# Four experts' results turned into rows by VectorE and transfers instead of TensorE, and the surplus plan moved into the last expert's phase

## The chip, the cores and the metric

The kernel runs on one core of a Trainium2 chip. The metric is device time in microseconds (us) of one execution; lower is better. The core's engines are TensorE (matrix products; its weight loads are listed apart as PEld), VectorE (DVE), ScalarE (ACT), GpSimd (POOL) and SyncE (SP), which here only issues transfers. Each engine works through its own instructions in order and waits for the others by semaphores.

## The reference, cut to what matters

Attention comes first, with a mask by hash buckets; it is untouched here. Its output, 3072 tokens of 512 numbers, goes through a mixture of eight experts. Each token is sent to the one expert with the largest logit:

```python
logits = x @ w_gate                      # x: 3072 x 512, 8 experts
expert_idx = np.argmax(logits, axis=1)
perm = np.argsort(expert_idx, kind='stable')
x_sorted = x[perm]
for e in range(8):
    lo, hi = boundaries[e], boundaries[e + 1]
    h = np.maximum(x_sorted[lo:hi] @ w1[e], 0.0)     # 512 -> 1024
    y_sorted[lo:hi] = h @ w2[e]                      # 1024 -> 512
y = y_sorted[inv_perm]
return gate_w[:, None] * y
```

## The kernel before

The first 400 us are attention and routing. They leave the tokens sorted by expert in a DRAM tensor (`sorted_rows`). What follows is a loop over phases `n` = 1 to 8 (phase 0 overlaps the end of attention). The experts are ranked by their number of tokens. Phases 0 and 1 are two halves, of 256 tokens, of the largest; phases 2 to 8 are the other seven, with room for 456, 432, 408, 396, 384, 372 and 354 tokens (`CAPS`). Tokens beyond that room are the surplus. A plan (`spill_plan`: some 46 small VectorE instructions, written as a generator that is advanced step by step) lists them in a small DRAM table, and a loop at the very end, run as many times as the plan says, works them off.

A phase has two parts. In the first, `mm1(n, f)` for f = 0 to 7 makes 128 hidden features of all the tokens: 12 products, since numbers are split into a high and a low part and three of the four combinations are summed. ScalarE writes the relu's high part (`relu("u")`), VectorE its low part (`relu("d")`), both out of one of three PSUM buffers (`s`). In the second part, `mm2(n, m)` for m = 0 to 3 multiplies by the second weights. Phases with at most 384 tokens are `by_token`: there a product's result has tokens in its rows and can be multiplied by the gate and scattered to the output (`yout`). In phases 2 to 5 the result comes out turned, with 128 output features in the rows and tokens in the columns. ScalarE copies it to the tile `yt`, and in the next phase's first part, after every second `mm1`, TensorE turns 128 tokens of it by four transposes (line 889), VectorE multiplies by the gate (line 894) and GpSimd scatters the rows by an indirect transfer (line 896).

Beside this the next expert is prepared. `halves` calls `chunk_part` once for each `mm1` and twice for each `mm2`: ScalarE rounds 512 columns of raw weights to their high part (line 718), GpSimd subtracts for the low part (line 719), and after each second part SyncE issues the load of another half chunk of raw weights (line 705), three halves ahead of its use. `rows` loads the next expert's tokens (line 735), 32 rows at a time, and `xt_blocks` turns them by VectorE's transposes of 32 x 32 blocks (line 773). The order on each engine is the order in which the program is written.

Of the kernel before, what the change touches and what calls it, by code (L numbers as in the profile page):

```python
# [7 lines left out]
F32 = mybir.dt.float32  # L8
# [15 lines left out]
E = 8  # L24
# [29 lines left out]
@with_exitstack  # L54
def lsh_attention_moe(ctx, tc, qk, qk2, v, proj, wg, w1, w1p, w2, out):
    nc = tc.nc
# [543 lines left out]
    def spill_plan():  # L600
# [18 lines left out]
        nc.vector.tensor_tensor(over, C["cnt"], cap, op=OP.subtract)  # L619
        gt = m2.tile([128, E, 21], F32, name="gt")  # L620
        yield
# [54 lines left out]
        nc.vector.tensor_scalar(tab[:, :, 1], et, float(E - 1), None, op0=OP.min)  # L676
        nc.sync.dma_start(tabd.rearrange("t p c -> p t c"), tab)
        cnt = const.tile([1, 1], I32, name="spn")
# [8 lines left out]
    def raw_load(c, a):  # L687

        r, k = divmod(c, 4)
        if k < 2:  # L690
            src = (w1p if r else w1)[bass.ds(EV[r], 1)].rearrange("o (a p) f -> p (o a) f", p=128)[:, 2 * a:2 * a + 2,
                                                                                k * 512:(k + 1) * 512]
        else:
            o = (k - 2) * 4 + 2 * a
            src = w2[bass.ds(EV[r], 1)].rearrange("o (a p) d -> p (o a) d", p=128)[:, o:o + 2, :]
        n = 2 * c + a
        if n in (2, 3):
            if n == 2:
                RAW["x"] = moe.tile([128, 2, 2, 512], F32, name="xhe")
            t = RAW["x"][:, a]  # L700
        elif n < 10 or n % 2:
            t = moe.tile([128, 2, 512], F32, name="raw", bufs=2)
        else:
            t = P2["p"].tile([128, 2, 512], F32, name="raw2", bufs=2)
        nc.sync.dma_start(t, src)
        RAW[c, a] = t
# [137 lines left out]
    def mm2(n, m, mid=None):  # L844

        r, o, c = PH[n]
        if by_token(n):
            yout(n, m, mid)
            return
        if m == 0:  # L850
            YT[n] = (wk.tile([128, 4, EARLY], F32, name="qk") if n == 0 else
                     P2["p"].tile([128, 4, CAPS[1]], F32, name="yt"))
        h = HH[n]
        ms = slice(m * 128, (m + 1) * 128)
        p = ps.tile([128, 512], F32, name="s", bufs=3)
        k = 0
        for f in range(8):
            w = CH[4 * r + 2 + f // 4]
            for a, b in ((0, 0), (0, 1), (1, 0)):
                nc.tensor.matmul(p[:, :c], w[:, a, f % 4, ms], h[b][:, f, :c], start=(k == 0), stop=(k == 23))  # L860
                k += 1
                if k == 12 and mid:
                    mid()
        nc.scalar.activation(YT[n][:, m, :c], p[:, :c], AF.Copy)

    def yout(n, j, mid=None):
# [4 lines left out]
        if n + 1 == len(PH) and j + 1 == len(tiles_of(c)):  # L871
            youts(n, j, i, pw)
            return
        p = ps.tile([128, 512], F32, name="s", bufs=3)
        if by_token(n):
            k = 0
            for f in range(8):
                w = CH[4 * r + 2 + f // 4]
                for a, b in ((0, 0), (1, 0), (0, 1)):
                    nc.tensor.matmul(p[:pw], HH[n][b][:, f, i:i + pw], w[:, a, f % 4],  # L880
                                     start=(k == 0), stop=(k == 23))
                    k += 1
                    if k == (12 if n else 20) and mid:
                        mid()
        else:

            yw = max(pw, min(128, CAPS[1] - i))
            for m in range(4):
                nc.tensor.transpose(p[:yw, m * 128:(m + 1) * 128], YT[n][:, m, i:i + yw], ident)  # L889
        if n:  # L890
            y = P2["p"].tile([128, DM], F32, name="y", bufs=3)
        else:
            y = moe.tile([128, DM], F32, name="y0")
# [8 lines left out]
    def youts(n, j, i, pw):  # L902

        r = PH[n][0]
        y = P2["p"].tile([128, DM], F32, name="y", bufs=3)
        ix = P2["p"].tile([128, 2], I32, name="ix2")
# [274 lines left out]
    for n in range(1, len(PH)):  # L1181
        c0 = 4 * (PH[n][0] + 1)
        last = n + 1 == len(PH)
        if not last:
            rows(n + 1)
        for f in range(8):
            mm1(n, f)
            if f % 2 and not by_token(n - 1):
                yout(n - 1, f // 2)
            halves(c0, f)  # L1190
            if 3 <= n < 6:
                for _ in range(2):
                    next(plan, None)
        for m in range(4):
            if not last:
                xt_blocks(n + 1, ((0, 1), (2,), (3,), ())[m] if not by_token(n) else ((0, 1), (2, 3), (), ())[m])
            if not (last and m == 3):
                mm2(n, m)
            halves(c0 + 2, 2 * m)
            halves(c0 + 2, 2 * m + 1)  # L1200
        if n == 6:
            for _ in plan:
                pass
        if n == 7:
            C["n"] = nc.values_load(C["cntn"][0:1, 0:1], min_val=0, max_val=TMAX)
    p2.close()
# [67 lines left out]
```

## Time and profile before

| | |
|---|---|
| median of three runs | 699.95 us (699.9 to 700.3) |
| the profiled execution | 699.71 us |
| its span, first to last instruction | 697.8 us |
| granted TensorE clock | 0.999 of full speed |
| TensorE busy | 688.8 us, 99% of the span |
| VectorE, ScalarE, GpSimd busy | 64%, 62%, 67% |

A share of busy time is an average over the whole span; what a change is worth is read from the stretch in which it is made, here from about 440 us to the end.

### The profile page before, as it was taken

The page shows a single profiled execution, that of the slowest core. Times are in us where ns is not written, and L with a number is a line of the kernel's source. Part 1 is how long each engine was busy: PE and PEld are TensorE (multiplying, and loading weights), DVE is VectorE, ACT ScalarE, POOL GpSimd, SP SyncE. Part 2 cuts the span into 40 slices and gives each one's busy share as a digit, 9 for nine tenths or more (in the row PEclk, how much of TensorE's full clock was granted, in tenths as well). Part 3 has the DMA queues.
Part 4 walks back from the last instruction along what each step waited for, and adds up shares of the span by engine and source line. Part 5 has one row for each costly group of instructions (what it writes and reads, how often), then busy time and mean ns, then how long its engine had stood idle before and what let it go on. Part 6 is the DMA issues. An engine that isn't in the chain of part 4 may idle for free.

```text
span 697.8 us, 12285 instructions
## 1 busy us (share of the span) xinstructions
PE 688.8 (99%) x4219; PEld 564.7 (81%) x4219; DVE 444.6 (64%) x916; ACT 434.3 (62%) x866; POOL 466.8 (67%) x517
## 2 busy tenths in 40 slices
PE   8999999999999999999999999999999999999997
PEld 4778677867786778677876789899999999989896
DVE  8878787878787878788875645342939333363421
ACT  7988888878888888887876315443443444444310
POOL 7967755595796768876866436856666676758522
PEclk9999999999999999999999999999999999999999
DMA  7609777976778558764983158656355493738101
GB/s 285 160 19 261 208 219 210 269 187 219 254 230 222 154 132 224 223 202 143 257 274 129 65 184 248 170 177 155 127 163 170 131 181 123 210 124 234 61 10 42
DMA packets 64528, 123.09 MB, mean 176 GB/s; under 512 B 15329, under 2 KB 29025, under 8 KB 64400
## 3 DMA queue, kind: packets, MB, share of 16 engines
q1 hardware_dynamic: 56736, 103.17, 52.2%
q0 software_dynamic: 7584, 19.10, 8.6%
q8 instruction: 34, 0.56, 0.3%
q14 instruction: 30, 0.25, 0.1%
q10 hardware_dynamic: 144, 0.02, 0.0%
HBM read 65.75 MB, written 26.33 MB: 132 GB/s over the span
## 4 chain that ended last, share of the span: by engine, by line
PE 92%; issue 4%; POOL 1%; ACT 1%; DVE 1%; POOLq 0%
PE s L823 19%; PE t L389 18%; PE s L860 11%; PE s L297 10%; PE t L327 10%; PE s L299 9%; PE s L880 8%; PE t L409 3%; PE t L254 2%; PE s L889 1%; POOL w L719 1%; PE t L103 1%; ACT e L313 0%; POOL out_dram L896 0%; ACT pt L379 0%
## 5 line engine op out<-in xcount | busy, mean ns | idle before, releaser
L307 DVE TENSOR_SCALAR_CACHE_REDUCE e<-s 128x768 f32<-128x768 f32 x192 | 178.9, 953 | 61.3 <-PE s L299 56.5
L313 ACT ACTIVATE e<-e,m 128x768 f32<-128x768 f32 x192 | 177.9, 929 | 16.3 <-DVE e L307 12.4
L719 POOL TENSOR_TENSOR w<-raw,w 128x512 fp32r<-128x512 f32 x112 | 144.6, 1314 | 36.7 <-ACT w L718 35.5
L389 PE MATMUL t<-pt,vt 128*64 128x384 f32 x768 | 130.9, 490 | 0.0
L823 PE MATMUL s<-xh,w 128*128 128x456 f32 (+6 forms) x672 | 126.8, 346 | 0.0
L823 PEld LDWEIGHTS s<-xh,w 128*128 128x128 f32 x672 | 119.2, 188 | 3.0
L839 DVE SCALAR_TENSOR_TENSOR hh<-s,hh 128x256 fp32r<-128x256 f32 (+7 forms) x64 | 35.5, 555 | 107.5 <-ACT hh L837 107.5
L389 PEld LDWEIGHTS t<-pt,vt 128*64 128x64 f32 x768 | 52.3, 137 | 63.7 <-issue 63.2
L327 PE MATMUL t<-ident,e 128*128 128x128 f32 x648 | 92.1, 274 | 1.4 <-DVE pt L377 0.5
L379 ACT ACTIVATE pt<-t 128x512 f32<-128x512 f32 (+1 forms) x147 | 82.1, 581 | 16.4 <-PE t L327 15.3
L837 ACT ACTIVATE hh<-s 128x256 fp32r<-128x256 f32 (+7 forms) x64 | 31.3, 490 | 90.7 <-PE s L823 90.7
L327 PEld LDWEIGHTS t<-ident,e 128*128 128x128 f32 x648 | 76.6, 140 | 8.7 <-ACT e L313 1.8
L349 DVE STREAM_TRANSPOSE w<-e 128x768 f32<-128x768 f32 x84 | 79.0, 964 | 0.8 <-DMA pt<-w 0.6
L896 POOL DMA_INDIRECT out_dram<-y,ix x28 | 27.9, 996 | 73.1 <-DVE y L894 43.9
L860 PE MATMUL s<-hh,w 128*128 128x456 f32 (+3 forms) x384 | 74.9, 355 | 0.0
L860 PEld LDWEIGHTS s<-hh,w 128*128 128x128 f32 x384 | 71.1, 188 | 2.6
L718 ACT ACTIVATE w<-raw 128x512 fp32r<-128x512 f32 x112 | 66.3, 622 | 1.0 <-DMA raw<-in_w1p_dram 1.0
L880 PE MATMUL s<-w,hh 128*128 128x512 f32 (+1 forms) x240 | 56.4, 394 | 0.0
L297 PE MATMUL s<-w 80*128 80x384 f32 x192 | 55.1, 368 | 0.0
L297 PE MATMUL s<-qk 80*128 80x384 f32 x192 | 54.8, 367 | 0.0
L880 PEld LDWEIGHTS s<-w,hh 128*128 128x128 f32 (+1 forms) x240 | 44.6, 187 | 10.5
L299 PE MATMUL s<-qk 128*128 128x384 f32 x192 | 49.8, 340 | 0.0
(220 smaller groups left out, 979.9 us busy)
## 6 DMA issues: line engine op xcount, KB each, us to landing
pt<-w SPq DMA_DIRECT2D x224, 144.0 KB, 3.8
raw<-in_w_dram SPq DMA_DIRECT2D x34, 512.0 KB, 3.4
raw<-in_w1p_dram SPq DMA_DIRECT2D x28, 512.0 KB, 3.4
xd<-in_qk_dram SPq DMA_DIRECT2D x14, 768.0 KB, 7.1
sorted_rows<-xr SPq DMA_DIRECT2D x6, 1156.0 KB, 8.1
vt<-in_v_dram SPq DMA_DIRECT2D x16, 384.0 KB, 3.8
masks<-bits POOLq DMA_DIRECT2D x14, 192.0 KB, 3.8
sorted_rows<-sorted_rows SPq DMA_DIRECT2D x2, 1156.0 KB, 7.1
```

The costliest lines, as they stand in the source:

```text
L297: nc.tensor.matmul(p[:, a, :HALF], k[0:80, 2, c], k[0:80, 3, n], start=i >= 4, stop=i < 4)
L299: nc.tensor.matmul(p[:, a, :HALF], k[:, 0, c], k[:, 1, n], start=i < 4, stop=i >= 4)
L307: nc.vector.tensor_scalar(e, SC.pop(i)[:, :, :HALF], CEIL, None, op0=OP.min, op1=OP.min, accum_out=m)
L313: nc.scalar.activation(e, e, AF.Exp, bias=m, scale=-1.0, accum_out=SM[g, hf][:, t, s:s + 1])
L327: nc.tensor.transpose(o[:, j, w], e[w][:, kt // 3, (kt % 3) * 128:(kt % 3) * 128 + 128], ident)
L349: nc.vector.transpose(z[:, :, c, w].rearrange("p g (k i) -> p g k i", i=32), e)
L379: nc.scalar.activation(o, x, AF.Copy)
L389: nc.tensor.matmul(p[s * 64:(s + 1) * 64, :HALF], VT[g][:, kt, s, :], PT[u][:, :, :, s, kt].rearrange("p a t i -> p t a i"), start=(kt == ...
L719: nc.gpsimd.tensor_tensor(w[:, 1, a], r, w[:, 0, a], op=OP.subtract)
L823: nc.tensor.matmul(p[:, :c], w[:, a, d, fs], x[:, b, d, :c], start=(k == 0), stop=(k == 11))
L860: nc.tensor.matmul(p[:, :c], w[:, a, f % 4, ms], h[b][:, f, :c], start=(k == 0), stop=(k == 23))
L880: nc.tensor.matmul(p[:pw], HH[n][b][:, f, i:i + pw], w[:, a, f % 4], start=(k == 0), stop=(k == 23))
```

## The change

In phases 2 to 5 the turning of the results leaves TensorE. After each `mm2` VectorE turns the copy `yt` by 32 x 32 blocks into a new tile `yb`. Such a transpose moves nothing between groups of 32 partitions; that is left to 16 transfers (`y_rows`), each from 32 partitions of `yb` to 32 of a new tile `yr`, in pieces of 512 bytes. SyncE issues two of them after each of the next phase's eight `mm1`. For the pieces to be whole, these four experts' second weights are read from a new input `w2p` with permuted columns. The multiplication by the gate now reads and writes `yr` in place, and it and the scatter stand in the next phase's second part, one behind each `mm2`. GpSimd clears the last columns of `yt` once a phase. The fourth block of the next expert's tokens is turned one `mm2` earlier.

The surplus plan was advanced by two steps behind each `mm1` of phases 3 to 5 and finished after phase 6. It is now advanced by six steps behind each of the last six `mm1` of phase 8; its table is stored after that phase's first `mm2`, and the number of turns is read by all the engines after its second.

```diff
@@ spill_plan
-        gt = m2.tile([128, E, 21], F32, name="gt")
+        gt = m2.tile([128, E, 24], F32, name="le2")[:, :, :21]
...
-        nc.sync.dma_start(tabd.rearrange("t p c -> p t c"), tab)
+        C["tab"] = tab
@@ raw_load
-            src = w2[bass.ds(EV[r], 1)].rearrange("o (a p) d -> p (o a) d", p=128)[:, o:o + 2, :]
+            src = (w2 if r == 0 or by_token(r + 1) else w2p)[bass.ds(EV[r], 1)].rearrange("o (a p) d -> p (o a) d", p=128)[:, o:o + 2, :]
@@ mm2
+        nb = -(-c // 32)
         if m == 0:
-            YT[n] = (wk.tile([128, 4, EARLY], F32, name="qk") if n == 0 else
-                     P2["p"].tile([128, 4, CAPS[1]], F32, name="yt"))
+            YT[n] = P2["p"].tile([128, 4, CB * 32], F32, name="yt")
+            YB[n] = P2["p"].tile([128, CB, 128], F32, name="yb")
+            nc.gpsimd.memset(YT[n][:, :, c:nb * 32], 0.0)
...
         nc.scalar.activation(YT[n][:, m, :c], p[:, :c], AF.Copy)
+        nc.vector.transpose(YB[n][:, :nb, 32 * m:32 * m + 32], YT[n][:, m, :nb * 32].rearrange("p (b j) -> p b j", j=32))
+
+    YB, YR = {}, {}
+
+    def y_rows(n, k):
+
+        nb = -(-PH[n][2] // 32)
+        if k == 0:
+            YR[n] = P2["p"].tile([128, 4, DM], F32, name="yr")
+        for i in (2 * k, 2 * k + 1):
+            r, a = divmod(i, 4)
+            q = (a + r) % 4
+            t = len(range(q, nb, 4))
+            nc.sync.dma_start(YR[n][32 * q:32 * q + 32, :t, 128 * a:128 * a + 128], YB[n][32 * a:32 * a + 32, q::4][:, :t])
@@ yout
-        p = ps.tile([128, 512], F32, name="s", bufs=3)
         if by_token(n):
+            p = ps.tile([128, 512], F32, name="s", bufs=3)
...
         else:
-
-            yw = max(pw, min(128, CAPS[1] - i))
-            for m in range(4):
-                nc.tensor.transpose(p[:yw, m * 128:(m + 1) * 128], YT[n][:, m, i:i + yw], ident)
-        if n:
-            y = P2["p"].tile([128, DM], F32, name="y", bufs=3)
+            p = YR[n][:, j]
+        if not by_token(n):
+            y = p
+        elif n:
+            y = P2["p"].tile([128, DM], F32, name="y", bufs=2)
@@ the loop over phases
         for f in range(8):
             mm1(n, f)
-            if f % 2 and not by_token(n - 1):
-                yout(n - 1, f // 2)
             halves(c0, f)
-            if 3 <= n < 6:
-                for _ in range(2):
-                    next(plan, None)
+            if not by_token(n - 1):
+                y_rows(n - 1, f)
+            if last and f > 1:
+                go(plan, 6)
         for m in range(4):
             if not last:
-                xt_blocks(n + 1, ((0, 1), (2,), (3,), ())[m] if not by_token(n) else ((0, 1), (2, 3), (), ())[m])
+                xt_blocks(n + 1, ((0, 1), (2, 3), (), ())[m])
             if not (last and m == 3):
                 mm2(n, m)
+            if not by_token(n - 1):
+                yout(n - 1, m)
             halves(c0 + 2, 2 * m)
             halves(c0 + 2, 2 * m + 1)
-        if n == 6:
-            for _ in plan:
-                pass
-        if n == 7:
-            C["n"] = nc.values_load(C["cntn"][0:1, 0:1], min_val=0, max_val=TMAX)
+            if last and m == 0:
+                go(plan, 99)
+                nc.sync.dma_start(tabd.rearrange("t p c -> p t c"), C["tab"])
+            if last and m == 1:
+                C["n"] = nc.values_load(C["cntn"][0:1, 0:1], min_val=0, max_val=TMAX)
```

TensorE's order in the first products of phase 3, before (`xh` holds that expert's tokens, `w` its first weights, `yt` the turned result of phase 2; line 860 is the second products):

```order
L823 MATMUL s<-xh,w_5362 128x432 x24
L889 MATMUL s<-ident,yt 128x128 x4
L823 MATMUL s<-xh,w_5362 128x432 x24
L889 MATMUL s<-ident,yt 128x128 x4
L823 MATMUL s<-xh,w_5435 128x432 x24
L889 MATMUL s<-ident,yt 128x128 x4
L823 MATMUL s<-xh,w_5435 128x432 x24
L889 MATMUL s<-ident,yt 72x128 x4
```

In the changed program the four groups of transposes are gone there, and the same 96 products follow each other without a break.

SyncE's queue in phase 3 after the change, behind the load of the next tokens (`xg` is its last piece, `raw` the raw weights; line 880 is `y_rows`):

```order
L740 DMA xg<-sorted_rows 128x4x2
L880 DMA yr<-yb 32x4x128 x2
L705 ISA
L705 DMA raw<-in_w1p_dram 128x2x512
L880 DMA yr<-yb 32x4x128
L880 DMA yr<-yb 32x3x128
L880 DMA yr<-yb 32x4x128 x2
L705 ISA
L705 DMA raw_5735<-in_w2p_dram 128x2x512
```

Before, the loads of raw weights followed the line of `xg` directly; now the first of them stands behind two transfers of rows and each later one behind four.

VectorE's order in the first products of phase 8 after the change (line 839 is `relu("d")`, lines 625 to 644 are the plan):

```order
L839 SCALAR_TENSOR_TENSOR hh_7305<-s,hh_7304 128x354
L625 TENSOR_REDUCE spl<-le_7377 128x8
L627 COPY spl<-spl 128x8
L630 TENSOR_TENSOR spl<-spl 128x1 x4
L839 SCALAR_TENSOR_TENSOR hh_7305<-s,hh_7304 128x354
L630 TENSOR_TENSOR spl<-spl 128x1 x3
L640 TENSOR_TENSOR le<-spl,tf 128x192
L642 TENSOR_REDUCE ttt<-le 128x24
L644 TENSOR_TENSOR le<-le,spl 128x192
L839 SCALAR_TENSOR_TENSOR hh_7305<-s,hh_7304 128x354
```

Before, the eight relus of this phase stood there one after the other, and these plan rows stood in phases 3 to 5 (the storing of the table in phase 6).

## Rows read from the trace of the kernel before

**Rows 1.** The page: its engines, and the chain that ended last.

```profile
PE 688.8 (99%) x4219; PEld 564.7 (81%) x4219; DVE 444.6 (64%) x916; ACT 434.3 (62%) x866; POOL 466.8 (67%) x517
...
PE s L823 19%; PE t L389 18%; PE s L860 11%; PE s L297 10%; PE t L327 10%; PE s L299 9%; PE s L880 8%; PE t L409 3%; PE t L254 2%; PE s L889 1%; POOL w L719 1%; PE t L103 1%; ACT e L313 0%; POOL out_dram L896 0%; ACT pt L379 0%
```

**Rows 2.** Stretches: phase 3's first products, its second, phase 8's first.

```profile
core 0: us, PE busy (x) PEld busy (x) DVE busy (x) ACT busy (x) POOL busy (x), PEclk, DMA share, GB/s
478.79:499.29 20.50, 20.50 (x113) 19.47 (x112) 14.05 (x33) 9.10 (x18) 13.63 (x18) 1.00 0.67 183
499.29:518.27 18.98, 18.98 (x100) 18.15 (x97) 9.74 (x16) 7.57 (x15) 11.51 (x10) 1.00 0.36 117
660.45:676.03 15.58, 15.58 (x98) 15.58 (x96) 4.44 (x8) 3.27 (x7) 6.36 (x6) 1.00 0.05 11
```

**Rows 3.** The chain in order of time: start us, us, what.

```profile
478.95 4.71 PE s L823 x24
483.66 0.44 PE s L889 x4
...
499.54 18.89 PE s L860 x96
...
643.88 16.73 PE s L880 x72
```

**Rows 4.** Line 889's instructions: min/median/max ns, first and last start us.

```profile
L889 PE MATMUL s<-ident,yt x64: 270/272/275, 483.5 to 610.7; 128*128 128x128 f32 x48, 128*72 128x128 f32 x16
```

**Rows 5.** VectorE from 418 us, by line and shape: busy us, mean ns.

```profile
L894 DVE TENSOR_SCALAR y<-s,gate 128x512 f32<-128x512 f32 x21 | 15.6, 744 | 18.5 <-PE s L880 18.5
...
L773 DVE STREAM_TRANSPOSE xt<-xb 128x480 f32<-128x480 f32 x4 | 2.5, 650 | 0.0
```

**Rows 6.** VectorE in order of time: start us, us, instruction.

```profile
501.75 0.15 DVE L630 TENSOR_TENSOR spl<-spl 128x1 f32<-128x1 f32 x1
501.93 0.36 DVE L640 TENSOR_TENSOR le<-spl,tf 128x192 f32<-128x192 f32 x1
...
536.52 2.88 DVE L667 TENSOR_SCALAR ttt<-ttt,rof 128x24 f32<-128x24 f32 x1
...
666.99 0.53 DVE L839 SCALAR_TENSOR_TENSOR hh<-s,hh 128x354 fp32r<-128x354 f32 x1 [1.42 <-ACT hh L837]
```

**Rows 7.** GpSimd in order of time; in brackets idle time before.

```profile
483.88 0.16 POOL L110 IOTA kf_i<- 128x21 int32 x1
...
536.80 2.55 POOL L719 TENSOR_TENSOR w<-raw,w 128x512 fp32r<-128x512 f32 x2
...
663.04 5.03 POOL L719 TENSOR_TENSOR w<-raw,w 128x512 fp32r<-128x512 f32 x4
...
682.86 1.00 POOL L896 DMA_INDIRECT out_dram<-y,ix  x1 [14.75 <-DVE y L894]
...
691.29 0.98 POOL L923 DMA_INDIRECT out_dram<-y,ix  x1 [1.90 <-DVEq L1210]
```

**Rows 8.** SyncE's queue in order of time, start of phase 4.

```profile
522.16 0.39 SPq L705 DMA_DIRECT2D raw<-in_w1p_dram  x1
```

**Rows 9.** ScalarE in order of time, phase 4.

```profile
518.47 0.53 ACT L864 ACTIVATE yt<-s 128x432 f32<-128x432 f32 x1 [3.15 <-PE s L860]
...
535.89 0.62 ACT L718 ACTIVATE w<-raw 128x512 fp32r<-128x512 f32 x1
```

**Rows 10.** Transfers by tile: KB each, median us from issue to landing.

```profile
raw<-in_w1p_dram SPq DMA_DIRECT2D x28, 512.0 KB, 3.4
...
xb<-sorted_rows SPq DMA_DIRECT2D x8, 208.0 KB, 5.0
...
spill_rows<-tab SPq DMA_DIRECT2D x1, 24.0 KB, 9.1
```

**Rows 11.** The scatters of tile y, issue to landing.

```profile
DMA to landing us min/median/max: 1.9/2.8/8.8
```

**Rows 12.** The read of the number of turns: ns, start us.

```profile
L1205 PEldq TENSOR_LOAD <-spn x1: 484/484/484, 656.3 to 656.3; - x1
...
L1205 POOLq TENSOR_LOAD <-spn x1: 502/502/502, 661.7 to 661.7; - x1
```

More of the change, by code (lines that the diff above doesn't have):

```diff
@@ L54, in lsh_attention_moe @@
 @with_exitstack
-def lsh_attention_moe(ctx, tc, qk, qk2, v, proj, wg, w1, w1p, w2, out):
+def lsh_attention_moe(ctx, tc, qk, qk2, v, proj, wg, w1, w1p, w2, w2p, out):
     nc = tc.nc
@@ L904, in youts @@
         r = PH[n][0]
-        y = P2["p"].tile([128, DM], F32, name="y", bufs=3)
+        y = P2["p"].tile([128, DM], F32, name="y", bufs=2)
         ix = P2["p"].tile([128, 2], I32, name="ix2")
@@ L1262 @@
     w1 = np.ascontiguousarray(w1).reshape(E, DM, F)
+    w2p = np.ascontiguousarray(np.asarray(inputs["moe_w2"]).reshape(E, F, 4, 4, 32).transpose(0, 1, 3, 2, 4)).reshape(E, F, DM)
     pj, wg = pj.reshape(2 * D, 32), wg.reshape(2 * D, NP, 2 * E)
@@ L1265 @@
               "in_w1_dram": np.ascontiguousarray(inputs["moe_w1"]), "in_w1p_dram": w1,
-              "in_w2_dram": np.ascontiguousarray(inputs["moe_w2"])}
+              "in_w2_dram": np.ascontiguousarray(inputs["moe_w2"]), "in_w2p_dram": w2p}
     nc = bacc.Bacc("TRN2", target_bir_lowering=False, num_devices=1, dynamic_dma_scratch_size=2048)
```

## Prediction

> **What bounds the kernel now.** I read the page first. TensorE is busy for 99% of the span and holds 92% of the chain that ended last [rows 1], so the end moves with TensorE's own work, unless the change makes TensorE wait. The chain's lines then say where in the span to look: line 889, the transposes that the change takes out, stands among TensorE's lines with 1% [rows 1]. The view by stretches comes next. I cut it at the starts of the first products (line 823) and second products (line 860) of each phase. In every stretch the granted clock is 1.00 of 2.4 GHz and TensorE is busy for the whole stretch, while VectorE, ScalarE and GpSimd are each busy for well under it [rows 2]. A list of TensorE's waits from 418 us on is empty. So in this stretch of the program one microsecond less of TensorE work is one microsecond less of span, as long as the other engines stay ahead.
>
> **What is removed.** 64 transposes: four phases (3 to 6, each turning the result of the one before), four tiles of tokens each, four transposes a tile. Their price depends on the view. The list of instructions gives each 272 ns [rows 4], but matmuls overlap in the array, so durations can't be added. The chain counts each instruction by what it adds to the end: a group of four takes 0.44 us between two runs of 24 products that take 4.71 us [rows 3]. 16 such groups are 7.0 us. The stretches give a second reading. The first products of phase 3 (96 of 432 columns, with four groups) take 20.50 us and its second products (96 of 432 columns, without) 18.98 [rows 2]: 1.52 us a phase, 6.1 us for four. This reading is low, since it is cut at starts: the products behind the last group begin while it still drains. In the chain, which counts ends, the same two stretches are 499.54 - 478.95 = 20.59 us and 18.89 us [rows 3], 1.70 apart, or 6.8 us for four. I take 7.0 and keep 6.1 as the low bound.
> The Trainium skill (TensorE: Matmul & The Clock Gate, Part 4: PE-mode transpose) gives about 275 ns for a transpose in a kernel's context. The trace agrees on the duration (272 ns), but by that price the sum would be 64 x 0.272 = 17.4 us, and by the chain it is 7.0; the two stretches above, 1.5 us apart and not 16 x 0.272 = 4.4, decide for the chain.
>
> **What is added on VectorE.** 16 transposes of blocks of up to 480 columns in the second products. The like of them, on 128x480, takes 650 ns [rows 5]. Each waits for ScalarE's copy of the result (0.53 us [rows 9]). Behind the one after the last second product stand one multiplication by the gate and the next expert's first relu. The multiplication (744 ns out of PSUM [rows 5]) now reads and writes SBUF. Its price there isn't in the trace; I bound it from 0.2 us to 2.9 us. The upper end is a small instruction within SBUF that took 2.88 us [rows 6], while GpSimd ran two subtractions of weights from 536.80 for 2.55 us and both ended at 539.4 [rows 7]. At worst VectorE is free 0.53 + 0.65 + 2.9 = 4.1 us into the next phase and ends its first relu 0.6 us later, at 4.7. A group of 12 first products takes 4.71 / 2 = 2.35 us in phase 3 [rows 3] and 384/432 of that, 2.1, in phase 6; with three PSUM buffers the fourth group is the first to want that buffer, 3 x 2.1 = 6.3 us in. So it costs nothing, and 1.6 us of delay are left before it does.
> The Trainium skill (SBUF — State Buffer, Who interferes with whom) has VectorE and GpSimd lock one pair of ports, the second blocked until the first is done. The trace agrees at the pair of rows that end at 539.4. By that rule the 16 multiplications would lose up to 16 x 2.2 = 35 us of VectorE's time, and TensorE none of it as long as each loss ends within those 1.6 us.
>
> **What is added on SyncE.** 16 transfers in each of phases 3 to 6, 64 KB at most each, on the queue that also loads raw weights. The nearest transfers take 5.0 us to land (208 KB, pieces of 512 bytes), raw weights 3.4 [rows 10]. Together they are 4 MB more, in stretches where the DMA engines are busy for 0.67 and 0.36 of the time [rows 2]. The first two of a phase write the tile of rows that the phase before still scatters. In phases 4 to 6 this makes the queue wait until that last scatter has landed: 0.53 + 0.65 + 0.2 to 2.9 on VectorE, 1.0 for the scatter's issue [rows 7], 2.8 for its landing (8.8 at most [rows 11]), 5.2 to 13.9 us after the phase began. Behind stands a load of raw weights that is issued today 3.9 us after the start of phase 4 (522.16 - 518.27 [rows 2, 8]). ScalarE needs it for its copy at 535.89 [rows 9], 17.6 us in. With 3.4 us of landing it may be issued as late as 14.2. So the wait is hidden, by nearly all of its bound.
> The scatters move from the first products to the second, four a phase. GpSimd's work, 16 subtractions of 5.03 / 4 = 1.26 us [rows 7] and four scatters of 1.0, is 24 us of 39.5 in phase 3 (20.50 + 18.98 [rows 2]), as before. Some subtractions slip by a few microseconds, and their weights are wanted half a phase later. Price: nothing.
>
> **What is moved.** The surplus plan goes from phases 3 to 5 into the last one, phase 8, six steps behind each of its last six first relus, where it is about 46 small VectorE instructions. Undisturbed ones take 0.15 to 0.36 us [rows 6]; some 12 are of the dear kind, 8 are memsets, the rest cheap: about 9 us by this estimate. The plan starts once GpSimd has ended the last subtractions at 663.04 + 5.03 = 668.07 and three index rows of 0.16 [rows 7], 8 us after phase 8 began (660.45). A group of first products takes 15.58 / 8 = 1.95 us [rows 2], and today the third relu runs at 666.99 [rows 6], before that point. With 1 to 2 us of plan between two relus of 0.53 us, the fourth relu ends near 10.3 us, when its buffer is wanted at 11.7; the sixth near 14.0, wanted at 15.6; the eighth near 18.4. That one is wanted by the 23rd or 24th of the second products, and 72 of those take 16.73 us [rows 3]: 15.58 + 23 x 0.232 = 20.9. TensorE waits for none, with 1.4 us to spare at the tightest. The spill count is ready at 19.3. TensorE's queue reads it ahead of the last half tile's products, which start at 15.58 + 48 x 0.232 = 26.7; today it reads it (0.48 us) at 656.3, 4.1 us before the products at 660.45 [rows 12], hence not before 22.6. GpSimd's read (0.50 us [rows 12]) falls into its 1.90 us of waiting for the last half tile [rows 7]. The plan's table needs 9.1 us to land [rows 10], 19.4 + 9.1 = 28.5 us into a phase of 697.8 - 660.45 = 37 us. Price: nothing, and up to 3 us if the 9 us of plan are 13.
>
> **The sum.** 699.71 - 7.0 = 692.7 us for the profiled execution; the median of the runs lies 0.24 above it, so 692.9. I say 693.0.
>
> **The rivals.**
> *The plan eats part of it.* The tightest buffer has 1.4 us. If the first steps start later or take half as long again, TensorE waits 1 to 3 us in phase 8: 694 to 696 us. For it: the margin is small. Chance 0.10.
> *The plan costs more than the transposes gave.* This ends on the other side. If the small instructions are slow for another reason than GpSimd, so that one of each six takes 2.9 us as in [rows 6], the plan takes 9 + 6 x 2.7 = 25 us. From 8.1 us on, with five relus of 0.53, the eighth relu would end near 35.8, wanted at 20.9: TensorE waits 14.9 us, 707.9 us. It decides from about 17 us of plan on (8.1 + 17 + 2.7 = 20.9 + 7). Against it: the slow rows end with GpSimd's, and GpSimd idles from 668.1 to 682.86 [rows 7]. By the Trainium skill's rule on the ports (SBUF — State Buffer, Who interferes with whom) an idle GpSimd blocks nobody, so it too speaks against. Chance 0.02.
> *The loads come late.* If the wait for the scattered rows lasts beyond 14 us in each of phases 4 to 6, and relus queue behind ScalarE's late copy, TensorE loses what goes beyond two PSUM buffers (4.7 us): a wait of 22 us would cost about 3 us each, 9 in all: 702 us. At 19 to 21 us the gain is gone in parts, 694 to 700. Chance 0.03.
> *Each transpose is worth its whole duration.* 699.95 - 17.4 = 682.5 us. Chance 0.01; the stretches speak against it.
>
> **How the numbers follow.** My forecast (all hidden, 692.3 to 693.9) has 0.84, the rivals 0.16. The low bound of the removed work, 6.1 us, gives 693.9, and the rival of the plan reaches to 696. The range is 692.0 to 695.5. A difference of 0.2% (1.4 us) is about what a measurement can tell from no change. Faster: forecast, plan in part, most of the late loads, whole duration, 0.95. Same: part of the late loads, 0.02. Slower: plan at full price and the worst of late loads, 0.03.
>
> **What would show it.** Right: no row of line 889's kind; first products of phases 3 to 6 in 18.8, 18.0, 17.3 and 16.8 us; no wait of TensorE after 418 us; phase 8's first products in 15.58 us and the 37 us from their start to the end as before. Wrong: a wait of TensorE for VectorE's relu in phase 8; plan rows of 2 us with GpSimd idle; raw loads issued more than 14 us after a phase's start, with ScalarE's copies of weights waiting for them.

## The result and the profile after

The changed kernel takes **693.71 us** (median of 6 runs, 692.92 to 694.09) beside 700.13 us for the kernel before on the same chip: a ratio of 0.9906, 95% interval 0.9894 to 0.9919. It is 6.4 us faster. The profiled execution took 693.65 us with a span of 691.9 us. TensorE's list of waits from 410 us on is still empty.

The chain that ended last, in order of time, of the changed kernel (time, us, engine and line, instructions):

```profile
480.05 18.83 PE s L823 x96
498.88 18.89 PE s L862 x96
517.76 17.97 PE s L823 x96
535.74 17.92 PE s L862 x96
553.65 17.28 PE s L823 x96
570.94 17.33 PE s L862 x96
588.26 16.81 PE s L823 x96
605.07 16.67 PE s L896 x72
...
654.68 15.58 PE s L823 x96
```

The runs of 24 products with 0.44 us of transposes between them [rows 3] have become runs of 96 with nothing between. The four first products of phases 3 to 6 take 18.83, 17.97, 17.28 and 16.81 us; 18.8, 18.0, 17.3 and 16.8 were expected. Phase 8's first products take 15.58 us, as before. From the start of phase 3 to the end it is 691.9 - 480.05 = 211.85 us, where it was 697.8 - 478.95 = 218.85 [rows 3]: **7.00 us less**, the predicted term. The medians differ by 6.4 because the span ahead of this part isn't the same in every execution: phase 3 began 1.1 us later in this profile than in that of the kernel before, and the change takes nothing off TensorE there. A later profile of the same kernel (below) has a span of 691.2 us.

From the start of phase 8's first products to the end it is 691.9 - 654.68 = 37.2 us, as before (697.8 - 660.61).

VectorE's timeline of the changed kernel (start, us, line, operation, tiles): the added pair in phase 3, a dear multiplication, and the plan beside the fourth and the eighth relu of phase 8.

```profile
504.32 0.65 DVE L867 STREAM_TRANSPOSE yb<-yt 128x448 f32<-128x448 f32 x1 [0.69 <-DMA raw<-in_w2p_dram]
504.89 0.45 DVE L909 TENSOR_SCALAR yr<-yr,gate 128x512 f32<-128x512 f32 x1
...
550.29 2.28 DVE L909 TENSOR_SCALAR yr<-yr,gate 128x512 f32<-128x512 f32 x1
...
663.92 0.52 DVE L839 SCALAR_TENSOR_TENSOR hh<-s,hh 128x354 fp32r<-128x354 f32 x1
...
671.21 0.23 DVE L667 TENSOR_SCALAR ttt<-ttt,rof 128x24 f32<-128x24 f32 x1
671.64 0.52 DVE L839 SCALAR_TENSOR_TENSOR hh<-s,hh 128x354 fp32r<-128x354 f32 x1
...
672.46 0.13 DVE L679 CAST spn<-spl 1x1 int32<-1x1 f32 x1
```

The multiplications together (count, then shortest, median and longest in ns):

```profile
L909 DVE TENSOR_SCALAR yr<-yr,gate x16: 433/444/2404, 504.9 to 624.8; 128x512 f32<-128x512 f32 x12, 72x512 f32<-72x512 f32 x1, 48x512 f32<-48x512 f32 x1, 24x512 f32<-24x512 f32 x1
```

The transposes cost what their like did. The multiplication within SBUF takes 0.44 us in the median and up to 2.40, inside the bounds of 0.2 to 2.9. The plan's row of line 667, 2.88 us before [rows 6], takes 0.23 here. The fourth relu ends 663.92 + 0.52 - 654.52 (start of phase 8) = 9.9 us into the phase (10.3 expected), the eighth 17.6 (18.4), the spill count is ready 18.1 us in (19.3).

SyncE's timeline of the changed kernel, in phase 4:

```profile
525.69 1.25 SPq L880 DMA_DIRECT2D yr<-yb  x2
527.20 0.40 SPq L705 DMA_DIRECT2D raw<-in_w1p_dram  x1
```

Phase 4 begins at 517.6, so the wait for the scattered rows ends 8.1 us in (5.2 to 13.9 expected) and the load behind it is issued 9.6 us in (14.2 allowed). In phases 5 and 6 the wait ends 9.2 and 9.5 us in and the load is issued 10.7 and 11.0 us in. A transfer takes 0.63 us to issue.

GpSimd's timeline of the changed kernel, at the start of phase 5 and in phase 8:

```profile
557.90 8.97 POOL L719 TENSOR_TENSOR w<-raw,w 128x512 fp32r<-128x512 f32 x7
...
657.15 5.03 POOL L719 TENSOR_TENSOR w<-raw,w 128x512 fp32r<-128x512 f32 x4
```

In phase 8 GpSimd is through with its subtractions at 662.2 and comes to the plan's index rows, as forecast. What I had not foreseen is the row of phase 5: with the scatters in the second products, seven subtractions run in one piece at the start of the phase; in phase 4 it is five and in phase 6 nine. The kernel before ran them in groups of two, now and then three, in phases 3 to 6 (the pair at 536.80 in [rows 7]).

### The profile page after: what moved, and what is told of

The parts are those of the page before. It is cut to its first block, busy times and chain, and to the rows that moved or that the text cites. A ratio compares the mean times of both kernels' runs of the same rounds, so it can differ in the third digit from the quotient of the medians.

```text
span 691.9 us, 12280 instructions
## 1 busy us (share of the span) xinstructions
PE 682.5 (99%) x4155; PEld 559.0 (81%) x4155; DVE 445.8 (64%) x932; ACT 434.8 (63%) x866; POOL 464.7 (67%) x521
## 4 chain that ended last, share of the span: by engine, by line
PE 96%; ACT 1%; issue 1%; DVE 1%; POOL 0%; POOLq 0%
PE s L823 21%; PE t L389 19%; PE s L862 11%; PE s L297 10%; PE t L327 10%; PE s L896 10%; PE s L299 10%; PE t L409 3%; PE t L254 2%; PE t L103 1%; ACT e L313 0%; ACT pt L379 0%; DVE qk L218 0%; POOL out_dram L938 0%; ACT qk L237 0%
## 5 line engine op out<-in xcount | busy, mean ns | idle before, releaser
L719 POOL TENSOR_TENSOR w<-raw,w 128x512 fp32r<-128x512 f32 x112 | 142.4, 1298 | 31.7 <-ACT w L718 30.6
L823 PE MATMUL s<-xh,w 128*128 128x456 f32 (+6 forms) x672 | 123.8, 345 | 0.0
L299 PE MATMUL s<-w 128*128 128x384 f32 x192 | 49.5, 339 | 0.0
```

Source lines behind the costliest of these rows:

```text
L299: nc.tensor.matmul(p[:, a, :HALF], k[:, 0, c], k[:, 1, n], start=i < 4, stop=i >= 4)
L719: nc.gpsimd.tensor_tensor(w[:, 1, a], r, w[:, 0, a], op=OP.subtract)
L823: nc.tensor.matmul(p[:, :c], w[:, a, d, fs], x[:, b, d, :c], start=(k == 0), stop=(k == 11))
```

## The experiments

**The two parts of the change apart.** My theory at this point: TensorE's time falls by what the transposes cost it in the chain, and the plan costs nothing in either place. The rival: the plan has to move, or its move has an effect of its own. The first kernel has the plan back in phases 3 to 5:

```diff
-        C["tab"] = tab
+        nc.sync.dma_start(tabd.rearrange("t p c -> p t c"), tab)
...
-            if last and f > 1:
-                go(plan, 6)
+            if 3 <= n < 6:
+                for _ in range(2):
+                    next(plan, None)
...
```

> The changed kernel with the surplus plan put back where it stood (two steps behind each first product of phases 3 to 5, table stored after phase 6, number of turns read after phase 7). My theory: all of the gain is the 64 transposes, and the plan costs nothing in either place, so this is as fast as the changed kernel, 693.7 us within 0.6. Rival (the plan in phase 8 eats part of the gain): 692.0 to 692.7. Rival (the plan must leave, since VectorE now has more to do in phases 3 to 6): slower than 694.5, with waits of TensorE for VectorE there.

Measured: 704.65 us, ratio 1.0053 (1.0033 to 1.0073): slower than the kernel before, and 11 us above the changed one. TensorE waits in phases 4, 5 and 7. Its timeline in this kernel (in brackets the idle time before a row and what ended it):

```profile
527.32 9.25 PE L823 MATMUL s<-xh,w 128*128 128x408 f32 x48 [1.29 <-DVE hh L839]
554.33 8.80 PE L823 MATMUL s<-xh,w 128*128 128x396 f32 x48
564.80 8.90 PE L823 MATMUL s<-xh,w 128*128 128x396 f32 x48 [1.67 <-DVE hh L839]
```

VectorE's timeline at the same times:

```profile
520.81 5.97 DVE L644 TENSOR_TENSOR le<-le,spl 128x192 f32<-128x192 f32 x1
...
557.77 6.45 DVE L676 TENSOR_SCALAR tab<-ttt 128x24 int32<-128x24 f32 x1
...
564.20 1.50 DVE L839 SCALAR_TENSOR_TENSOR hh<-s,hh 128x396 fp32r<-128x396 f32 x3
```

And GpSimd's:

```profile
520.27 6.28 POOL L719 TENSOR_TENSOR w<-raw,w 128x512 fp32r<-128x512 f32 x5
...
557.90 7.64 POOL L719 TENSOR_TENSOR w<-raw,w 128x512 fp32r<-128x512 f32 x6
```

A row of the plan that takes 0.2 to 0.4 us alone stands there for 5.97 us while GpSimd runs five subtractions, and for 6.45 us beside five of the six in the second line: the sixth starts 0.09 us after the fifth has ended, and VectorE's row ends in that gap. Three relus queue behind it and then run in a row. Of phase 5's first products, four groups (48) run, and the fifth wants the PSUM buffer that the second relu holds: it waits 1.67 us.

That is a part of the loss. TensorE's waits in this execution add up to 6.4 us in six places, and the two behind plan rows are 3.0 of them. The other four come later, and the first stands behind ScalarE, which waits for raw weights. ScalarE's timeline and TensorE's, in phase 5:

```profile
577.43 0.63 ACT L718 ACTIVATE w<-raw 128x512 fp32r<-128x512 f32 x1 [5.35 <-DMA raw<-in_w1p_dram]
...
578.51 0.44 PE L862 MATMUL s<-hh,w 128*128 128x396 f32 x1 [1.01 <-ACT hh L837]
```

SyncE's timeline, what SyncE waited for behind it (total, times, longest), and a stretch after it (the last three numbers are the granted clock, the DMA engines' busy share and GB/s):

```profile
564.24 0.41 SPq L677 DMA_DIRECT2D spill_rows<-tab  x1
564.91 1.31 SPq L705 DMA_DIRECT2D raw<-in_w1p_dram  x1
...
SPq L880 <- DMA spill_rows<-tab: 5.0, 1, 5.0
...
566.00:572.00 6.00, 6.00 (x35) 6.00 (x34) 1.14 (x2) 2.47 (x5) 2.57 (x2) 1.00 0.93 13
```

The plan stores its table with its last steps. At two steps behind each first product, some 46 steps end in phase 5 and not in phase 6: in the kernel before the store is issued at 559.79, 3.9 us into phase 5. Here it is issued 9.9 us in, right behind the row of 6.45 us. For the six microseconds shown the DMA engines are busy and move 13 GB/s; ScalarE gets the raw weights 12.5 us after their load was issued (3.4 is the median landing [rows 10]), and the transfers of rows wait 5.0 us for the store to land. Measured from start to start, phase 4's and 5's first products are 1.55 and 1.93 us longer than in the changed kernel, phase 5's second and phase 7's first 1.71 and 3.05; these four make up all that the two executions differ by from phase 3 on. So the plan's old place costs in two ways, by the blocked rows and by its store in SyncE's queue. No run has the one without the other, and that phase 7's part is the store's delay handed on is argued, not shown. This execution took 701.23 us; the median is 3.4 us longer, and of those executions there is no trace. My theory's half on the plan fell.

The second kernel is the other part alone, the kernel before with the plan in phase 8:

```diff
...
-            if 3 <= n < 6:
-                for _ in range(2):
-                    next(plan, None)
+            if last and f > 1:
+                go(plan, 6)
...
```

> The kernel before with only the surplus plan moved to phase 8. My theory: 700.1 us, no change within 0.5; VectorE's plan rows take 0.13 to 0.36 us each, 9 us in all, and the eighth relu of phase 8 ends some 18 us after the phase began, without a wait of TensorE. Rival (the move costs): 701 to 703 us. Rival (the move gains by itself): below 699.4.

Measured: 700.55 us, ratio 1.0004 (0.9994 to 1.0013). Moving the plan gains nothing by itself. The parts don't add: +0.5% and 0.0% alone, -0.9% together.

**What a group of transposes costs.** The kernel before, each group of four done twice into the same place:

```diff
-            for m in range(4):
+            for m in (0, 1, 2, 3, 0, 1, 2, 3):
```

> The kernel before with each group of four transposes done twice, 64 more of them; the second result overwrites the first with the same numbers. By the price in the chain (0.44 us a group): 16 more groups, 7.0 us more, 707.1 us. By the mean duration of one (0.272 us): 17.4 us more, 717.5 us. By the low reading of the stretches (1.52 us a phase): 6.1 us more, 706.2.

Measured: 706.49 us, ratio 1.0088 (1.0073 to 1.0103), which is 6.5 us more; the span grew from 697.8 to 705.0, by 7.2. The chain that ended last in this kernel:

```profile
479.24 4.71 PE s L823 x24
483.95 0.87 PE s L889 x8
```

A group of eight counts 0.87 us where four counted 0.44 [rows 3]. 64 more of them cost 6.5 to 7.2 us, 0.10 to 0.11 us each, and not the 0.27 us that each lasts. The chain's price holds, and the rival of the whole duration (17.4 us) falls.

**Where else the plan could stand.** Two kernels put it, or GpSimd's work, so that they meet. The first moves the plan from phase 8's first products to those of phase 7:

```diff
-            if last and f > 1:
+            if n == 7 and f > 1:
                 go(plan, 6)
```

> The changed kernel with the surplus plan one phase earlier: six steps behind each of the last six first products of phase 7, the rest as in the change. In phase 7 GpSimd runs its subtractions of weights back to back from the phase's eighth microsecond to its twentieth, in phase 8 it idles there. The theory that the first call left (a plan row of VectorE that wants GpSimd's port waits for the whole unbroken run of subtractions, and the relus behind it hold TensorE): 5 us slower than the changed kernel or more, 698 to 708 us, with plan rows of several microseconds. Rival (what hurt there was the queue of transfers and loads in phases 3 to 6, not the port): 693.7 us within 1.

Measured: 705.35 us, ratio 1.0069 (1.0044 to 1.0095). TensorE's timeline in phase 7 of this kernel:

```profile
643.61 5.72 PE L823 MATMUL s<-xh,w 128*128 128x372 f32 x24 [10.74 <-DVE hh L839]
```

VectorE's, ahead of it:

```profile
637.79 3.86 DVE L115 CAST kf<-kf_i 128x21 f32<-128x21 int32 x1 [9.91 <-POOL kf_i L110]
```

And GpSimd's, which VectorE waits for:

```profile
631.48 6.16 POOL L719 TENSOR_TENSOR w<-raw,w 128x512 fp32r<-128x512 f32 x5
...
637.92 3.69 POOL L719 TENSOR_TENSOR w<-raw,w 128x512 fp32r<-128x512 f32 x3
```

The plan's index rows stand in GpSimd's queue behind a run of subtractions, and VectorE stands in its own queue for them, 9.9 us. Its first row then waits out the next run, 3.86 us. TensorE loses 10.7 us in one place, nearly all of the 11.9 between the two kernels. Behind the wait it was granted 0.50 of the clock in the first 2 us, and the 24 products shown took 5.72 us in place of about 4.1 (16.21 / 4 in the changed kernel).

The second leaves the plan in phase 8 and adds six subtractions within SBUF on GpSimd beside it (work that nothing reads):

```diff
...
+            if last and f == 2:
+                for _ in range(6):
+                    nc.gpsimd.tensor_tensor(busy[:, 8:12], busy[:, 0:4], busy[:, 4:8], op=OP.subtract)
```

> The changed kernel with six subtractions of 128x512 within SBUF on GpSimd, of numbers that nothing uses, right behind the plan's three index rows in phase 8 (some 7.6 us of GpSimd, 8 to 15.6 us into the phase, where it idles otherwise), and a small clearing before them. If VectorE's plan rows wait for GpSimd's work in SBUF: the first blocked row holds VectorE until 15.6, the fourth relu ends near 17 instead of 10, and TensorE, which wants that buffer at 11.7, waits 5 to 6 us: 699 to 700 us. If the long plan rows of the kernel before had another cause: 693.7 us and plan rows as short as now.

Measured: 699.04 us, ratio 0.9994 (0.9980 to 1.0007): 5.3 us of the gain are lost. GpSimd's timeline of this kernel in phase 8, with the added work:

```profile
663.20 8.04 POOL L1213 TENSOR_TENSOR yb<-yb 128x512 f32<-128x512 f32 x6
```

VectorE's, with a row of the plan and the relu behind it:

```profile
667.32 1.40 DVE L622 TENSOR_TENSOR le<-spl,kf 128x168 f32<-128x168 f32 x1
668.64 0.51 DVE L839 SCALAR_TENSOR_TENSOR hh<-s,hh 128x354 fp32r<-128x354 f32 x1
```

TensorE's, at the wait for that relu, and the stretch behind the wait:

```profile
669.20 6.64 PE L823 MATMUL s<-xh,w 128*128 128x354 f32 x24 [3.28 <-DVE hh L839]
...
669.20:673.00 3.80, 3.80 (x13) 3.80 (x14) 3.49 (x12) 0.00 (x0) 2.00 (x3) 0.50 0.00 0
```

Here a plan row lasts about one subtraction (1.34 us) and not the whole run, yet the sum is enough to make TensorE wait 3.28 us. The expected time came out, but not by the way that was expected (one row held for all six). The rest of the loss is the clock: behind the wait TensorE was granted 0.50, the level of 1.2 GHz, in the stretch shown, and the 24 products took 6.64 us, where a quarter of the changed kernel's 15.58 is 3.9. The Trainium skill (SBUF — State Buffer, Who interferes with whom) says that the engine that comes second is blocked for the whole instruction of the first. This run agrees with that; in the rows-only kernel the block lasted over five instructions, and there the measurement decides.

**Is it the scatters' place alone?** If so, the kernel before should become slow by moving its transposes, multiplications and scatters into the second products, with the plan left in phases 3 to 5:

```diff
...
-                     P2["p"].tile([128, 4, CAPS[1]], F32, name="yt"))
+                     P2["p"].tile([128, 4, CAPS[1]], F32, name="yt", bufs=2))
...
-            if f % 2 and not by_token(n - 1):
-                yout(n - 1, f // 2)
...
                 mm2(n, m)
+            if not by_token(n - 1):
+                yout(n - 1, m)
```

> The kernel before, with TensorE's transposes, the multiplication and the scatter of an expert's rows moved from the next expert's first products to its second ones (two buffers for the second products' results instead of one, nothing else moved; the plan stays in phases 3 to 5). If what spoiled the plan's old place is where the scatters stand (GpSimd's subtractions then run unbroken at the start of a phase, and a small row of VectorE waits for the whole run), this alone is slow, by the loss that the rows-only kernel showed against the changed one, 11 us: 707 to 713 us, with TensorE waiting for the second relu in phases 3 to 5, and no wait in phase 2. If the loss came from VectorE's transposes or the sixteen transfers: 699.5 to 700.5 us.

Measured: 701.45 us, ratio 1.0013 (1.0001 to 1.0025). About 1 us, not 11: the place of the scatters isn't the cause by itself. VectorE's timeline in phase 5 of this kernel:

```profile
559.86 3.78 DVE L676 TENSOR_SCALAR tab<-ttt 128x24 int32<-128x24 f32 x1
...
563.62 1.02 DVE L839 SCALAR_TENSOR_TENSOR hh<-s,hh 128x396 fp32r<-128x396 f32 x2
```

GpSimd's, the run that blocks it:

```profile
558.55 5.05 POOL L719 TENSOR_TENSOR w<-raw,w 128x512 fp32r<-128x512 f32 x4
```

TensorE's, the start of the phase:

```profile
556.33 17.53 PE L823 MATMUL s<-xh,w 128*128 128x396 f32 x96
```

The run is there and blocks the same row, for 3.78 us, but it is a run of four that ends 558.55 + 5.05 - 556.33 = 7.3 us into the phase. The second relu ends near 7.8 us and its buffer is wanted at 4 x 2.2 = 8.8 (a group takes 8.80 / 4 us in the rows-only kernel's row above). In the rows-only kernel the run of six ends 557.90 + 7.64 - 554.33 = 11.2 us in, and the second relu near 10.4. GpSimd frees itself at almost the same time in both (557.90 and 558.55), but TensorE without transposes is in phase 5 two microseconds earlier. So for this wait it takes both: the late scatters, and phases that are shorter by the 1.8 us of their transposes while GpSimd's work is as long as it was. That the late scatters alone don't suffice is measured; the part of the shorter phase I read from these two traces, and no run of its own tested it.

The later waits of the rows-only kernel are missing here too, though the table's store is as late (563.67) and ScalarE waits for the load behind it:

```profile
576.39 0.63 ACT L718 ACTIVATE w<-raw 128x512 fp32r<-128x512 f32 x1 [4.14 <-DMA raw<-in_w1p_dram]
```

TensorE loses 0.2 us by that. This kernel has no transfers of rows in SyncE's queue, so they are a second difference between the two, and no run tested it by itself either.

**The sixteen transfers.** First, all of them behind the second product instead of two behind each:

```diff
-            if not by_token(n - 1):
-                y_rows(n - 1, f)
+            if f == 1 and not by_token(n - 1):
+                for k in range(8):
+                    y_rows(n - 1, k)
```

> The changed kernel with all sixteen transfers of a phase issued behind the second of the first products instead of two behind each of eight. One load of raw weights then passes ahead of them and the next stands behind all sixteen, some 10 us of issue. My theory: it is hidden, 693.7 within 0.7. Rival (dealing them over the eight products is what makes it work): slower than 695, ScalarE waits for raw weights early in the second products.

Measured: 693.14 us, ratio 0.9894 (0.9879 to 0.9909), no wait of TensorE. Beside the changed kernel's 693.5, measured with it (below), this is no difference: dealing them out isn't needed.

Then each transfer issued twice, to the same place:

```diff
+            for _ in range(2):
-            nc.sync.dma_start(YR[n][32 * q:32 * q + 32, :t, 128 * a:128 * a + 128], ...)
+                nc.sync.dma_start(YR[n][32 * q:32 * q + 32, :t, 128 * a:128 * a + 128], ...)
```

> The changed kernel with each of the 64 transfers of rows issued twice, with the same contents. In the changed kernel SyncE needs about 0.63 us to issue one, so its queue gets 10 us longer in each of phases 3 to 6 and the loads of raw weights behind it slip by 0 to 10 us. My theory (the loads have that much to spare): within 1 us of the changed kernel, 693.5 to 694.7. Rival (the queue is already near its limit): each phase loses some microseconds, 698 us or more, with ScalarE's copies of weights waiting for transfers.

Measured: 833.78 us, ratio 1.19. It isn't the test that I meant, since the second of each pair waits for the first to land. SyncE's waits:

```profile
SPq L881 <- DMA yr<-yb: 116.1, 64, 4.1
```

64 waits of up to 4.1 us, 116 in all, are 29 us a phase in place of 10. So I repeated it with the second copy going to memory of its own, where nothing waits for it:

```diff
...
-            nc.sync.dma_start(YR[n][...], YB[n][...])
+            for d in (YR[n], copy[n]):
+                nc.sync.dma_start(d[...], YB[n][...])
```

> The changed kernel, each of the sixteen transfers of a phase followed by a second one of the same rows to a place of their own in device memory that nothing reads (an added copy; the output is untouched). Nothing waits for the copies, so SyncE's queue only grows by sixteen issues of about 0.63 us, 10.1 us a phase. If the loads and the turned rows have ten microseconds to spare (in phase 4 of the changed kernel SyncE's last load of the first part is issued 21.5 us into 36, and the queue then stands still for 7 us): 693.4 to 694.7 us, no waits of TensorE. If not: VectorE's first multiplication, which needs all sixteen, would end some 33 us into the phase instead of 25, the halves of the next expert's x behind it come late, and TensorE waits 2 to 3 us in each of four phases: 700 to 705 us.

Measured: 722.34 us, ratio 1.0307 (1.0288 to 1.0326), 28.8 us above the changed kernel's 693.5. The loads and the turned rows don't have ten microseconds to spare, and the loss is several times what I had given for that case. SyncE's timeline of this kernel, the last copy of phase 3:

```profile
506.02 0.59 SPq L882 DMA_DIRECT2D ycopy<-yb  x1
```

VectorE's, the first transpose of the next results, which overwrites yb, in phases 3 and 4:

```profile
508.79 0.65 DVE L867 STREAM_TRANSPOSE yb<-yt 128x448 f32<-128x448 f32 x1 [4.83 <-DMA ycopy<-yb]
...
553.55 0.61 DVE L867 STREAM_TRANSPOSE yb<-yt 128x416 f32<-128x416 f32 x1 [13.94 <-DMA ycopy<-yb]
```

GpSimd's, the first scatter of the turned rows:

```profile
510.08 1.00 POOL L913 DMA_INDIRECT out_dram<-yr,ix  x1 [8.30 <-DMA raw<-in_w2p_dram]
```

TensorE's, the start of phase 6:

```profile
601.54 20.00 PE L823 MATMUL s<-xh,w 128*128 128x384 f32 x96 [6.77 <-ACT yt L866]
```

SyncE's, the first load of raw weights after phase 3's scatter, and the first transfer of rows in phase 4:

```profile
513.68 9.87 SPq L705 DMA_DIRECT2D raw<-in_w1p_dram  x3
...
528.24 0.60 SPq L882 DMA_DIRECT2D yr<-yb  x1
```

The last copy of phase 3 is issued at 506.02, 25.8 us into the phase (it began at 480.2). VectorE, which must not write yb before it has been read, stands for 4.83 us (0.69 in the changed kernel). The next expert's x, which VectorE turns behind that, is late by it. GpSimd's scatter, put down to a load by the profile, goes 0.3 us after VectorE's multiplication, after 8.3 us of idling (4.2 in the changed kernel), with the subtractions behind it. Those free the raw weights' buffers, and SyncE's next load waits for GpSimd: it is issued 33.5 us into phase 3 (29.3 in the changed kernel), and phase 4's first transfer of rows 10.3 us into that phase (8.1). So the next phase starts with a queue that is later still, and there VectorE stands for 13.94 us. TensorE is held up from phase 5 on, at most for 6.77 us. A delay that one phase hides is handed on to the next by the ring from SyncE over VectorE and GpSimd back to SyncE. TensorE's listed waits come to 19.1 us of the 28.8. Part of the rest is the clock, by a stretch of the same trace (us, busy times, granted clock), the 4 us behind the longest wait:

```profile
601.54:605.50 3.96, 3.96 (x12) 3.69 (x13) 3.96 (x5) 3.84 (x8) 1.92 (x3) 0.50 0.34 118
```

Behind the wait TensorE was granted 0.50, the level of 1.2 GHz, and phase 6's first products took 20.00 us (the row of TensorE above), where the changed kernel's took 16.97 in the same view.

**A better version?** Expert 7's results (phase 7 of the plan, 372 columns) also turned by VectorE, their multiplications and scatters ahead of phase 8's second products; the changed kernel again beside it; and this variant together with all transfers at once.

```diff
-        return PH[n][2] <= 384
+        return PH[n][2] <= 384 and n != 7
...
```

> The changed kernel with phase 7 (372 tokens) turned in the same way as phases 2 to 5: its second products are 96 of 372 columns in place of 72 of 512, its sixteen transfers are dealt over phase 8's first products, and its three multiplications and scatters stand ahead of phase 8's second products. My theory (TensorE's rows alone set the time): 96 products of 372 columns took 16.21 us as first products, the 72 took 16.73, so 0.5 us faster than the changed kernel run beside it. Rival: VectorE, which has three transposes, the plan and three multiplications more around phase 8's start, delays the relus there, or the extra scatters delay the last ones: the same or slower than the changed kernel by up to 3 us.

> The changed kernel itself, beside the others of this call. Both theories: 693.7 us within 0.6. Its trace from the first product of phase 2 to the end is 251.8 us, 7.0 less than before; what precedes it, 439 to 440 us, varies from run to run without a cause in the change.

> The changed kernel with two variants that ran before at once: all sixteen transfers behind the second product, and the eighth phase's x results (expert 7 of the plan, the last but one phase) also turned by VectorE instead of being computed by rows. Each alone measured 693.1 and 693.5 us beside 693.5 for the changed kernel. If their small savings add: 692.9 to 693.2 us; if they are nothing: 693.3 to 693.7. No wait of TensorE in either case.

Measured: 693.5 us (ratio 0.9909, 0.9890 to 0.9930), 693.5 (0.9905, 0.9890 to 0.9919) and 693.88 (0.9903, 0.9887 to 0.9920). None beats the changed kernel. The 0.5 us that fewer columns should have given phase 7's second products is not there: 96 products of 372 columns took 16.57 us, 72 of 512 took 16.73. So one of 372 columns took 172.6 ns there, and why stays open.

## Why the prediction was right

**The bound and the removed work** were right, to the size: TensorE has no gap, the first products took what was worked out, and 7.00 us are gone between phase 3 and the end. The doubled transposes give the same price the other way round.

**VectorE's added work** lay in its bounds and was hidden. Twelve multiplications on 128x512 took 809 ns in the mean, between 0.44 and 2.40 us, for the reason given (GpSimd's subtractions beside them).

**SyncE's wait** ended 8.1 to 9.5 us into phases 4 to 6, inside 5.2 to 13.9. What I named as its danger, a late load of raw weights, was not the whole of it: the longer queue shows that the first thing to be late are VectorE's rows that need the transfers read or landed, and everything in order behind them. The rival of the late loads was priced at 9 us for a wait of 22 us; a queue about 10 us longer cost 28.8 us, because the phases pass the delay on.

**"Price: nothing" for the scatters and the slipped subtractions** holds for this kernel only. I took GpSimd's work as a sum, 24 us of 39.5, "as before"; it had changed its shape, from groups of two to runs of five to nine at the starts of phases 4 to 6, and a run blocks VectorE's small rows. What keeps the price at nothing is the other edit, the plan whose rows no longer stand beside those runs and whose store is no longer ahead of loads in SyncE's queue (the description of the change puts that store in phase 6; it stood in phase 5). I priced the edits one by one and missed that one needs the other, so that this price came out right is luck: the plan's move is worth 0 us in the kernel before and 11 us here.

**The plan in phase 8** went as worked out, with every time within 1.2 us of the forecast and on its early side. The rival that it costs more than the transposes gave didn't happen, and the busy GpSimd shows what it would have needed: six subtractions there took 5.3 us back, about half of it by the clock.

## What to carry to other kernels

Price a removed instruction on a pipelined engine by the gap that it leaves between its neighbours in the chain, not by its duration. When an edit moves work on an engine that shares something with another, look at the length of the unbroken runs that it makes there, not only at the sum, and try the edits apart: two that are worth nothing or less alone can be worth all of it together. A queue that is hidden needs a margin that is measured, since a delay beyond it was handed from phase to phase here.

## What the runs showed of the hardware

- A VectorE row within SBUF of 24 to 192 columns was held while GpSimd ran subtractions back to back: 5.97 us beside five, 6.45 beside five, 3.78 beside the last three of four. In the busy-GpSimd kernel it was let in after about one (1.1 to 1.4 us). The six subtractions there follow each other every 1.34 us and last 1.28, so there is a gap between them; the five of 6.28 us follow every 1.26 and last 1.31, so each begins before the one ahead has ended. In these traces a gap let the row in each time. Without one it was mostly held, but not always: in the kernel before the row of line 676 ended after 0.44 us, between the second and the third of three such subtractions. So what decides isn't settled. The relu of the busy-GpSimd kernel, which reads PSUM and one tile in SBUF, took 0.51 us in the middle of such a run.
- Waits of TensorE of 2.57, 3.28, 6.77 and 10.74 us were followed by stretches granted 0.50 to 0.52 of the clock (the level of 1.2 GHz); behind the waits of 1.3 and 1.7 us of the rows-only kernel the granted clock was 1.00.
- Four transposes of 128 columns between two runs of products cost 0.44 us [rows 3], though each lasts 272 ns [rows 4].
- The store of the plan's table, 24 KB, took 9.1 us to land in the kernel before [rows 10], and in the rows-only kernel the DMA engines were busy for 0.93 of a stretch behind it and moved 13 GB/s.
- In the kernel with each transfer issued twice to the same tile, SyncE's queue waited for the first to land, up to 4.1 us, before it went on. Whether the chip needs that wait or only the program asks for it, no run here shows.
